# Gated convolution and GELU MLP, forward and backward: the MLP bias by full-row products or by ScalarE, smaller PSUM groups, and buffers laid out anew

## The chip, the cores and the metric

The kernel runs on one core of one Trainium2 chip. The metric is device time in microseconds for one execution, forward and backward together. TensorE is called PE below (PEld is its weight load), VectorE DVE, ScalarE ACT, GpSimd POOL, and SP is the engine whose queue issues most DMAs.

## What is computed

Four layers in a row on x of 2048 tokens by 512 channels, in bf16, and then all gradients of the chain. Layers 0 and 2 are a gated long convolution, layers 1 and 3 a GELU MLP; each acts on the layer norm of x and is added to x:

```
k_shift = 4-tap causal convolution of k;   kv = k_shift * v
A(n) = n * (causal convolution of kv with ssm_k, by FFT, + kv * ssm_D)
B(n) = gelu(n @ w1 + b1) @ w2 + b2          # w1 512x1376, w2 1376x512
x = x + A(ln(x)); x = x + B(ln(x)); x = x + A(ln(x)); x = x + B(ln(x))
out, grads = vjp of that chain for q, k, v, shift_k, ssm_k, ssm_D, w1, b1, w2, b2
```

A has the same k, v and filter in both layers, so its convolution is computed once.

## The kernel before, in words

The program has three stages. **The forward convolution** (`phase_conv_forward`) makes cosine and sine tables, turns k, v and the filter into spectra by products with the tables, multiplies them on DVE and transforms back; its result y stays in SBUF as `y_res`. At its end DVE adds y into x and sums the statistics of the first layer norm; POOL makes their reciprocal root (`rstd`, `nmr`).

**The MLP stage** (`phase_mlp`, L1605 on) takes x through all four layers and back. The tokens are cut into 8 blocks of 256 (`block_steps`); in each block there are two MLP layers forward (numbers 1 and 3) and two backward, so 16 block-layers each way. The hidden 1376 is padded to 11 chunks of 128. Forward (`mlp_layer`, L1213): ACT applies the norm (`l_n`), SP turns it by DMA (`l_nT`), PE forms each chunk in PSUM (`mm_ps`) with four products over 512 channels and a fifth that adds the bias, ACT copies the chunks to `l_g`, ACT and DVE compute gelu and its derivative in pieces of 6 and 5 chunks, the derivative goes to DRAM (`gp_d`), the hidden layer `l_h` goes to DRAM (`h_d`), and PE forms the second product in `oo_ps`. Before the change the fifth product has a contraction of one row: the weights are the row `b1` (`b_row` in the trace) and the moving operand a row of ones (`b_ones`):

```
for dc in range(ND):
    b_.nc.tensor.matmul(v, lhsT=w.w1[:, dc, cs], rhs=nT[:, dc, :], start=(dc == 0), stop=False)
b_.nc.tensor.matmul(v, lhsT=w.b1[:, cs], rhs=w.ones, start=False, stop=True)
```

The chunks are grouped by `ZG` (L1101): 3, 3, 3 and 2 chunks share a PSUM tile of 1024 columns, of which there are two, and one ACT copy takes a group out. Backward (`backward_layer`, L1297) works likewise with `w2T` and `w1T`, turned copies of the weights that `turn_steps` (L1105) makes at the stage's start, and ends each block with corrections of the layer norm on DVE, POOL and ACT; the last gradients of a block leave by SP (`out_dram`, `o1B_d`).

The order of that stage is not that of the code. `Plan` collects all steps with an estimated duration, a latency, and what they read and write; `Plan.order` (L1025) then places them one by one, each time the step that can start first by these estimates (ties by a rank with the constant `LEAN`), and hands out buffers from `SLOTS` (L1601). The program is emitted in that order, and each engine keeps its own.

**The rest** is the backward convolution (`conv_backward`) with the weight gradients (`weight_grads`) as a filler between its steps: it reads h from DRAM turned by DMA (`dw_tm`, 16 pieces of 128x128 each, `fetch` at L1485; the first five stand alone at L1534) and forms 22 sums of 32 products (`dw_ps`). The convolution loads its table (`tabFb`) and spectra (`Hb`, `KVb`); PE runs 61 products of `dw_ps` and then the first of the convolution (`sp_ps`). Tiles wait for whatever last used their place in SBUF, so where a tile lies decides what it waits for.

Of the kernel before, what the change touches and what calls it, by code (L numbers as in the profile page):

```python
# [16 lines left out]
P = 128  # L17
# [119 lines left out]
def build_consts(nc, tc, const_pool):  # L137
    c = Consts()
    with tc.tile_pool(name="c_tmp", bufs=1) as tp:
# [28 lines left out]
        nc.vector.memset(c.onescol_f, 1.0)  # L168
        c.pibias = const_pool.tile([P, 1], F32, name="pibias")
# [547 lines left out]
def conv_backward(ctx, nc, tc, dims, consts, dram, res, aps):  # L717
# [18 lines left out]
    with tc.tile_pool(name="cb_tabF", bufs=1, side="right", reuse_waits="tile") as tp:  # L736
        tabF = []
        for x, w in ((0, 512), (512, 1536)):
            tabF.append(tp.tile([P, 2, 2, w], BF16, name=f"tabFb{x}"))
            nc.scalar.dma_start(out=tabF[-1], in_=dram.tabF[:, :, :, x:x + w])  # L740
# [245 lines left out]
class Plan:  # L986
# [38 lines left out]
    def order(self, prio, ready_at, free):  # L1025
# [9 lines left out]
        open_ = {k: [(0.0, i) for i in range(n)] for k, n in self.slots.items()}  # L1035
# [21 lines left out]
        while len(out) < len(self.steps):  # L1057
# [29 lines left out]
def act_t(n, psum=False, cols=0):  # L1087
    return 0.05 + 0.835e-3 * n + 0.05 * psum + 0.1 * cols
# [6 lines left out]
def ts_t(n):  # L1095
    return 0.01 + 0.295e-3 * n
# [4 lines left out]
ZG = ((0, 3), (3, 3), (6, 3), (9, 2))  # L1101
EG = ((0, 6), (6, 5))


def turn_steps(p, m, E, A, consts):  # L1105

    D, ND, NFC, w = m.D, m.ND, m.NFC, m.w
    for dc in range(ND):
# [14 lines left out]
    for c in range(NFC):  # L1123
# [12 lines left out]
        E(1.1, mm, -1, 0, writes=[ps])  # L1136
        A(act_t(512, True), ev, -1, 0, reads=[ps], part=[("w1T",)])


def block_steps(p, m, dram, b, E, A, V, G, S, go_ap, out0, out1, forward):  # L1140
# [20 lines left out]
    def stats(l):  # L1161
        for i, t in enumerate(tl):
# [3 lines left out]
            V(0.68, f, b, l, reads=[X], part=[("mv", b)])  # L1166
# [7 lines left out]
        G(2.3, g, b, l, reads=[("mv", b)], writes=[("rs", b, l)])  # L1174
# [12 lines left out]
    def turned(N, key, l, src, hold, after=()):  # L1187
        for i in range(T):
# [3 lines left out]
            S(1.28, f, b, l, lat=1.7, reads=[N] if N else [], part=[key], hold=hold, after=after)  # L1192
# [20 lines left out]
    def mlp_layer(l):  # L1213
# [3 lines left out]
        hold = ("GE", b, l)  # L1217
# [4 lines left out]

        for c0, k in ZG:
            ps, gi = ("mm", b, l, c0), int(c0 >= EG[1][0])
            for c in range(c0, c0 + k):
                def f(b_, c=c, c0=c0, ps=ps):
# [51 lines left out]
        for i in range(T):  # L1278
# [18 lines left out]
    def backward_layer(l, first):  # L1297
# [16 lines left out]
        for gi, (g0, k) in enumerate(EG):  # L1314
            S(0.5, lambda b_, gi=gi, g0=g0, k=k, l=l, Q=Q: b_.nc.sync.dma_start(
                out=b_(Q[gi])[:, 0:k * HB], in_=m.gp_d[l][:, b, g0 * HB:(g0 + k) * HB]), b, st, lat=3.0,
              reads=[("gpd", b, l)], writes=[Q[gi]], after=[fed], hold=hold)
        for c0, k in ZG:
            ps = ("mm", b, l, c0, "B")
            for c in range(c0, c0 + k):  # L1320
# [6 lines left out]
                E(0.432, f, b, st, reads=[NT_, ("w2T",)], part=[ps], hold=hold)  # L1327
# [3 lines left out]
            A(act_t(k * HB, True), f, b, st, reads=[ps], part=[H + (int(c0 >= EG[1][0]),)], hold=hold)  # L1331
        H2 = [H + (0,), H + (1,)]
# [402 lines left out]
```

## Time and profile before

| | before |
|---|---|
| median of 3 runs (lowest to highest) | 950.11 us (945.30 to 954.85) |
| profiled execution, its own time | 939.36 us |
| its span in the trace | 937.6 us |
| busy: PE, DVE, ACT, POOL | 819.6, 744.1, 572.6, 185.8 us |
| granted TensorE clock, mean | 0.952 of full speed |

The span is the time from the first to the last instruction in the trace. A busy share is an average over stages with different limits. In rows of the timeline, the first number is the start and the second the duration; x4 means four instructions in one row, whose duration is from the start of the first to the end of the last. A row's bracket says how long the engine had been idle before it, and what ended that.

### The profile page before, as it was taken

The page shows a single profiled execution, that of the slowest core. Times are in us where ns is not written, and L with a number is a line of the kernel's source. Part 1 is how long each engine was busy: PE and PEld are TensorE (multiplying, and loading weights), DVE is VectorE, ACT ScalarE, POOL GpSimd, SP SyncE. Part 2 cuts the span into 40 slices and gives each one's busy share as a digit, 9 for nine tenths or more (in the row PEclk, how much of TensorE's full clock was granted, in tenths as well). Part 3 has the DMA queues.
Part 4 walks back from the last instruction along what each step waited for, and adds up shares of the span by engine and source line. Part 5 has one row for each costly group of instructions (what it writes and reads, how often), then busy time and mean ns, then how long its engine had stood idle before and what let it go on. Part 6 is the DMA issues. An engine that isn't in the chain of part 4 may idle for free. (4 is left out here: it accounts for less than half of the span.)

```text
span 937.6 us, 14102 instructions
## 1 busy us (share of the span) xinstructions
PE 819.6 (87%) x5282; PEld 452.2 (48%) x5282; DVE 744.1 (79%) x1289; ACT 572.6 (61%) x718; POOL 185.8 (20%) x329
## 2 busy tenths in 40 slices
PE   4778789348799999999999999786899998898997
PEld 4453334124343445555556566552344445765664
DVE  9865798962997877978997887787359999899774
ACT  7776645246778889788786765442433326754664
POOL 5401110110431210313231312222000122310000
PEclk9999989758896999999999999999999999999999
DMA  6788766031543455748576779959959999884321
GB/s 220 263 283 321 251 247 225 0 79 34 148 150 105 130 191 138 225 147 247 150 214 207 229 204 271 276 165 227 291 143 279 216 330 327 262 287 112 97 78 39
DMA packets 210030, 183.04 MB, mean 195 GB/s; under 512 B 94950, under 2 KB 184233, under 8 KB 209578
## 3 DMA queue, kind: packets, MB, share of 16 engines
q1 hardware_dynamic: 194762, 135.70, 50.8%
q0 software_dynamic: 11968, 40.15, 11.9%
q10 hardware_dynamic: 3232, 6.29, 1.8%
q8 instruction: 41, 0.67, 0.3%
q14 instruction: 27, 0.22, 0.1%
HBM read 86.32 MB, written 82.13 MB: 180 GB/s over the span
## 5 line engine op out<-in xcount | busy, mean ns | idle before, releaser
L55 ACT ACTIVATE l_g<-l_g 128x1536 bf16<-128x1536 bf16 (+1 forms) x96 | 128.7, 1370 | 5.2 <-DVE l_g L55 4.6
L55 PE MATMUL mm_ps<-l_nT,w_sb 128*128 128x256 bf16 x704 | 116.4, 292 | 3.4 <-ACT l_g L55 1.9
L55 PEld LDWEIGHTS <-l_h 128*128 128x128 bf16 x704 | 67.5, 99 | 99.5 <-DVE l_h L55 12.9
L55 PEld LDWEIGHTS <-dw_tm 128*128 128x128 bf16 x704 | 66.9, 99 | 83.5 <-DMA dw_tm<-h_d 8.0
L55 PEld LDWEIGHTS <-w_sb 128*128 128x128 bf16 x836 | 70.0, 102 | 70.0 <-issue 38.9
L55 PE MATMUL oo_ps<-w_sb,l_h 128*128 128x512 bf16 x352 | 85.3, 392 | 12.0 <-ACT w1T_sb L55 9.2
L55 PE MATMUL dw_ps<-G,dw_tm 128*128 128x512 bf16 x352 | 86.2, 384 | 7.3 <-DMA dw_tm<-h_d 3.7
L55 PE MATMUL dw_ps<-x_sl,dw_tm 128*128 128x512 bf16 x352 | 86.0, 385 | 3.5 <-DMA dw_tm<-h_d 3.5
L55 PE MATMUL mm_ps<-l_nT,w2T_sb 128*128 128x256 bf16 x704 | 82.2, 273 | 7.4 <-DMA l_nT<-goB_d 3.7
L55 DVE TENSOR_TENSOR l_g<-l_g,l_g 128x1536 bf16<-128x1536 bf16 (+1 forms) x96 | 83.5, 887 | 0.9
L55 PE MATMUL oo_ps<-w1T_sb,l_h 128*128 128x512 bf16 x352 | 80.0, 379 | 4.3 <-DVE l_h L55 4.2
L55 PEld LDWEIGHTS <-w2T_sb 128*128 128x128 bf16 x704 | 68.3, 98 | 21.9 <-issue 4.3
L55 ACT ACTIVATE l_g<-mm_ps 128x768 bf16<-128x768 f32 x64 | 48.3, 754 | 49.4 <-PE mm_ps L55 49.1
L55 ACT ACTIVATE l_h<-mm_ps 128x768 bf16<-128x768 f32 x64 | 47.6, 753 | 31.8 <-PE mm_ps L55 22.5
L55 DVE TENSOR_SCALAR l_g<-l_g 128x1536 bf16<-128x1536 bf16 (+1 forms) x64 | 33.3, 520 | 37.7 <-ACT l_g L55 37.7
L1506 ACT ACTIVATE dw_tm<-dw_tp 128x1024 bf16<-128x1024 bf16 x44 | 44.6, 1024 | 27.2 <-PE dw_tp L55 24.4
L55 PE MATMUL mm_ps<-b_ones,b_row 1*128 1x256 bf16 x176 | 51.3, 291 | 8.5 <-POOL b_ones L1628 8.5
L55 DVE TENSOR_REDUCE b1a<-dw_fm 128x1 f32<-128x2048 bf16 x22 | 49.6, 2277 | 0.0
L55 ACT ACTIVATE l_n<-x_sl,nmr,rstd 128x512 bf16<-128x512 bf16 x48 | 37.1, 806 | 18.4 <-POOL nmr L978 16.0
L55 POOL TENSOR_SCALAR l_dg<-ident,b_cols 128x128 bf16<-128x128 bf16 x32 | 25.5, 796 | 106.7 <-DVE b_junk L55 106.7
L1565 ACT ACTIVATE dw_o<-dw_ps 128x512 bf16<-128x512 f32 x22 | 13.1, 597 | 54.4 <-PE dw_ps L55 34.5
L55 ACT ACTIVATE l_n<-l_n,b_cols 128x512 bf16<-128x512 bf16 x32 | 24.8, 806 | 26.6 <-POOL b_cols L55 26.6
(296 smaller groups left out, 1559.6 us busy)
## 6 DMA issues: line engine op xcount, KB each, us to landing
h_d<-l_h SPq DMA_DIRECT2D x16, 704.0 KB, 4.8
gz_d<-l_h SPq DMA_DIRECT2D x16, 704.0 KB, 5.4
dw_fm<-gz_d SPq DMA_DIRECT2D x22, 512.0 KB, 9.0
l_n<-n_d SPq DMA_DIRECT2D x36, 256.0 KB, 5.0
n_d<-l_n SPq DMA_DIRECT2D x24, 256.0 KB, 3.3
gp_d<-l_g SPq DMA_DIRECT2D x16, 384.0 KB, 3.3
l_g<-gp_d SPq DMA_DIRECT2D x16, 384.0 KB, 3.8
gp_d<-l_g SPq DMA_DIRECT2D x16, 320.0 KB, 3.2
```

Of the source, the lines that this page charges most:

```text
L55: return self.tc.keep_in_program_order(f(*args, **kwargs))
L1506: nc.scalar.activation(out=dst, in_=ps, func=ACT.Identity)
L1565: nc.scalar.activation(out=o, in_=ps, func=ACT.Identity)
```

## The change

1. **Bias.** `BIAS_ROWS` names 9 of the 16 forward block-layers (layer 1 of blocks 0 to 4, layer 3 of blocks 0 to 3). There the fifth product stays, now with a full contraction: its weights are 128 rows of which the first is b1 and the rest zero, its moving operand a 128x256 tile of ones. In the other 7 it is gone, and ACT adds the bias while it copies, chunk by chunk, from a column `b1col`. The rows are cleared by ACT, and the column is made by 11 products of one column each; both are steps of the plan.
2. **PSUM groups.** `ZG` has groups of 2, 2, 2, 2, 2 and 1; `mm_ps` is four tiles of 512 columns. This holds for backward layers too.
3. **The plan.** Estimated durations are replaced; rank gets a number for each stage (`DELAY`); slots can be held back at the start (`LATE`) and are chosen by their number; `SLOTS` changes; some dependencies are narrowed.
4. **Places in SBUF.** The tiles of the MLP stage are laid out one by one in an order of their own. `tabFb` moves to the left side of SBUF, and `dw_t3`, `dw_t6` are taken last.

The diff, cut to what is spoken of:

```diff
+        c.ones = const_pool.tile([P, HB], BF16, name="ones")
+        nc.vector.memset(c.ones, 1.0)
...
-    with tc.tile_pool(name="cb_tabF", bufs=1, side="right", reuse_waits="tile") as tp:
+    with tc.tile_pool(name="cb_fold", bufs=1, side="right", reuse_waits="tile") as tp, \
+            tc.tile_pool(name="cb_tabF", bufs=1, reuse_waits="tile") as tabp:
...
-        open_ = {k: [(0.0, i) for i in range(n)] for k, n in self.slots.items()}
+        open_ = {k: [(LATE.get((k, i), -100.0), i) for i in range(n)] for k, n in self.slots.items()}
...
-ZG = ((0, 3), (3, 3), (6, 3), (9, 2))
+ZG = ((0, 2), (2, 2), (4, 2), (6, 2), (8, 2), (10, 1))
 EG = ((0, 6), (6, 5))
+BIAS_ROWS = {(b, 1) for b in range(5)} | {(b, 3) for b in range(4)}
...
+    def clear(b):
+        for f in range(0, FP, 256):
+            k = min(256, FP - f)
+            b.nc.scalar.activation(out=w.b1[:, f:f + k], in_=consts.nyq[:, 0:k], func=ACT.Copy, scale=0.0)
+        b.nc.scalar.activation(out=w.b1[0:1, F:F + 1], in_=consts.nyq[0:1, 0:1], func=ACT.Copy, scale=PAD_H)
...
+            b.nc.tensor.matmul(ps[:, c:c + 1], lhsT=w.b1[:, c * P:(c + 1) * P], rhs=consts.ones[:, 0:1], start=True, stop=True)
...
-                        b_.nc.tensor.matmul(v, lhsT=w.w1[:, dc, cs], rhs=nT[:, dc, :], start=(dc == 0), stop=False)
-                    b_.nc.tensor.matmul(v, lhsT=w.b1[:, cs], rhs=w.ones, start=False, stop=True)
-                forward.append(E(0.54, f, b, l, reads=[NT_], part=[ps], hold=hold))
+                        b_.nc.tensor.matmul(v, lhsT=w.w1[:, dc, cs], rhs=nT[:, dc, :], start=(dc == 0),
+                                            stop=(dc == ND - 1 and not by_row))
+                    if by_row:
+                        b_.nc.tensor.matmul(v, lhsT=w.b1[:, cs], rhs=consts.ones, start=False, stop=True)
+                forward.append(E(0.57 if by_row else 0.455, f, b, l, reads=[NT_, ("b1",)], part=[ps], hold=hold))
...
+                if by_row:
+                    b_.nc.scalar.activation(out=z, in_=v[:, 0:k * HB], func=ACT.Identity)
+                    return
+                for c in range(k):
+                    cs = slice(c * HB, (c + 1) * HB)
+                    b_.nc.scalar.activation(out=z[:, cs], in_=v[:, cs], func=ACT.Identity, bias=w.b1col[:, c0 + c:c0 + c + 1])
...
-    spare, held = [f"dw_t{x}" for x in range(7)], {}
+    spare, held = [f"dw_t{x}" for x in (0, 1, 2, 4, 5, 3, 6)], {}
...
-SLOTS = {"n": 5, "nT": 4, "h": 5, "g": 16, "u": 2, "gx": 5, "g1": 3, "dg": 4, "mm": 2, "oo": 4}
+SLOTS = {"n": 5, "nT": 4, "h": 5, "g": 17, "u": 2, "gx": 4, "g1": 1, "dg": 4, "mm": 4, "oo": 4}
-LEAN = 8.0
+LEAN = 10.7
+DELAY = (-0.2, 5.5, -10.9, 0.5, -1.8, -6.8, -0.8, 2.3, 6.2, 12.6)
...
-        nc.gpsimd.memset(m.w.ones, 1.0)
-        nc.gpsimd.memset(m.w.b1[:, F:NFC * P], 0.0)
-        nc.gpsimd.memset(m.w.b1[:, F:F + 1], PAD_H)
...
-        tiles["mm"] = [psum.tile([P, 1024], F32, name=f"mm_ps{i}") for i in range(SLOTS["mm"])]
+        tiles["mm"] = [psum.tile([P, 512], F32, name=f"mm_ps{i}") for i in range(SLOTS["mm"])]
```

What this does to the engines' orders shows at two places. The first is ACT at the start of the MLP stage, from the last copy of the forward convolution (`W`) on; `w2T_sb` are the copies of turned weights, `l_n` the first two norms. Before:

```order
L371 ACTIVATE W_1389<-iv_ps 128x512
L55 ACTIVATE l_n_1933<-x_sl,nmr_101,rstd_98 128x512 x2
L55 ACTIVATE l_n_1934<-x_sl,nmr_101,rstd_98 128x512 x2
L55 ACTIVATE w2T_sb<-oo_ps_1979 128x1024
L55 ACTIVATE w2T_sb<-oo_ps_1980 128x1024
L55 ACTIVATE w2T_sb<-oo_ps_1981 128x1024
L55 ACTIVATE w2T_sb<-oo_ps_1982 128x1024
L55 ACTIVATE w2T_sb<-oo_ps_1979 128x384
```

The same place on ACT in the changed kernel, where `b_rows` is the clearing of the bias rows:

```order
L373 ACTIVATE W_1391<-iv_ps 128x512
L55 ACTIVATE b_rows<-nyq 128x256 x5
L55 ACTIVATE b_rows<-nyq 128x128
L55 ACTIVATE b_rows<-nyq 1x1
L55 ACTIVATE w2T_sb<-oo_ps_1971 128x1024
L55 ACTIVATE w2T_sb<-oo_ps_1972 128x1024
L55 ACTIVATE w2T_sb<-oo_ps_1973 128x1024
L55 ACTIVATE w2T_sb<-oo_ps_1974 128x1024
L55 ACTIVATE w2T_sb<-oo_ps_1971 128x384
```

The clearing and the copies of turned weights, seven of which stood behind the first norms, now all stand ahead of them. The second place is SP's queue at the end of the MLP stage, before:

```order
L55 DMA gz_d<-l_h_1945 1408x1x256
L55 DMA l_n_1937<-n_d 128x2x512
L55 DMA out_dram<-l_n_1935 128x2x512
L1491 DMA_TRANSPOSE dw_tm<-h_d 128x16x128 x5
L55 DMA o1B_d<-l_n_1937 128x2x512
L55 DMA_TRANSPOSE dw_tm<-h_d 128x16x128 x3
```

And the same end of SP's queue in the changed kernel:

```order
L55 DMA gz_d<-l_h_1962 1408x1x256
L55 DMA l_n_1958<-n_d 128x2x512
L55 DMA out_dram<-l_n_1956 128x2x512
L55 DMA o1B_d<-l_n_1958 128x2x512
L1525 DMA_TRANSPOSE dw_tm<-h_d 128x16x128 x5
L55 DMA_TRANSPOSE dw_tm<-h_d 128x16x128 x3
```

The store of the last block's gradient (`o1B_d`) moved ahead of the first five turned loads of h.

## Rows read from the trace of the kernel before

**Rows 1.** Busy time by stretch: span; PE, PEld, DVE, ACT, POOL busy (count); clock; DMA.

```profile
186.00:205.00 19.00, 5.21 (x25) 2.55 (x25) 15.68 (x31) 7.71 (x11) 3.03 (x8) 0.50 0.39 97
205.00:240.00 35.00, 26.21 (x139) 12.67 (x139) 12.36 (x18) 24.22 (x26) 0.00 (x0) 0.74 0.12 32
240.00:545.00 305.00, 294.83 (x1761) 159.45 (x1760) 253.45 (x456) 242.87 (x284) 76.78 (x124) 0.97 0.60 178
545.00:641.00 96.00, 83.38 (x530) 50.70 (x529) 77.78 (x182) 48.88 (x66) 22.70 (x48) 1.00 0.81 228
641.00:664.00 23.00, 17.34 (x66) 7.13 (x67) 11.96 (x15) 2.12 (x3) 4.17 (x7) 0.85 1.06 279
664.00:938.00 274.00, 257.93 (x1841) 148.74 (x1839) 223.18 (x322) 136.92 (x199) 36.67 (x49) 1.00 0.70 201
```

**Rows 2.** Waits of DVE and ACT from 240 to 641 us: total, times, longest.

```profile
DVE l_g L55 <- ACT l_g L55: 20.4, 18, 2.6
...
ACT l_g L55 <- PE mm_ps L55: 28.1, 28, 3.8
```

**Rows 3.** Timeline of PE: two forward chunks, and a backward layer's 44 products.

```profile
219.91 0.61 PE L55 MATMUL mm_ps<-l_nT,w_sb 128*128 128x256 bf16 x4
...
220.66 0.61 PE L55 MATMUL mm_ps<-l_nT,w_sb 128*128 128x256 bf16 x4
...
575.73 4.97 PE L55 MATMUL mm_ps<-l_nT,w2T_sb 128*128 128x256 bf16 x44
580.53 0.59 PE L55 MATMUL oo_ps<-l_n,l_dg 128*128 128x512 bf16 x2
```

**Rows 4.** Timeline and groups of ACT by shape: count | busy us, mean ns | idle.

```profile
239.80 2.02 ACT L55 ACTIVATE w1T_sb<-oo_ps 128x512 bf16<-128x512 f32 x4
...
L55 ACT ACTIVATE l_g<-mm_ps 128x768 bf16<-128x768 f32 x48 | 38.7, 807 | 38.8 <-PE mm_ps L55 38.5
L55 ACT ACTIVATE l_n<-x_sl,nmr,rstd 128x512 bf16<-128x512 bf16 x48 | 37.1, 806 | 18.4 <-POOL nmr L978 16.0 <-POOL nmr L55 2.3
L55 ACT ACTIVATE l_g<-mm_ps 128x512 bf16<-128x512 f32 x16 | 9.6, 597 | 10.6 <-PE mm_ps L55 10.6
...
L893 ACT ACTIVATE Wh<-gh_ps 128x257 bf16<-128x257 f32 x24 | 8.0, 386 | 3.6 <-PE gh_ps L55 3.6
```

**Rows 5.** Timeline of the MLP stage's start, several engines.

```profile
186.59 2.93 ACT L55 ACTIVATE l_n<-x_sl,nmr,rstd 128x512 bf16<-128x512 bf16 x4 [16.01 <-POOL nmr L978]
...
192.56 1.06 PE L55 MATMUL mm_ps<-l_nT,w_sb 128*128 128x256 bf16 x4
...
199.28 2.74 DVE L55 TENSOR_TENSOR y_res<-W 128x512 bf16<-128x512 bf16 x8
...
202.08 0.37 PE L55 MATMUL mm_ps<-b_ones,b_row 1*128 1x256 bf16 x1 [8.46 <-POOL b_ones L1628]
...
211.27 0.56 DVE L55 TENSOR_SCALAR l_g<-l_g 128x1536 bf16<-128x1536 bf16 x1 [9.25 <-ACT l_g L55]
...
240.42 3.92 PE L55 MATMUL oo_ps<-w_sb,l_h 128*128 128x512 bf16 x11 [9.21 <-ACT w1T_sb L55]
```

**Rows 6.** Timeline of the MLP stage's end: SP's queue, PE, DVE.

```profile
637.63 16.24 SPq L1491 DMA_TRANSPOSE dw_tm<-h_d  x5
...
643.20 5.01 PE L55 MATMUL dw_ps<-G,dw_tm 128*128 128x512 bf16 x16 [3.73 <-DMA dw_tm<-h_d]
...
646.70 0.69 DVE L55 TENSOR_TENSOR l_n<-l_u,l_n 128x1024 bf16<-128x1024 bf16 x1 [1.06 <-ACT l_n L55]
...
658.58 4.67 PE L55 MATMUL dw_ps<-x_sl,dw_tm 128*128 128x512 bf16 x13 [3.46 <-DMA dw_tm<-h_d]
663.05 1.92 PE L55 MATMUL sp_ps<-fold_t,tabFb 128*128 128x512 bf16 x8
```

**Rows 7.** Busy time in two stretches of 5 us, columns as in rows 1.

```profile
285.00:290.00 5.00, 5.00 (x21) 2.11 (x20) 3.51 (x5) 4.68 (x6) 0.63 (x3) 0.50 0.43 110
...
585.00:590.00 5.00, 1.29 (x8) 0.44 (x6) 4.93 (x13) 0.00 (x0) 2.52 (x3) 1.00 1.23 299
```

More of the change, by code (lines that the diff above doesn't have):

```diff
@@ L1068, in order @@
                 if n not in held:
-                    open_[n[0]].sort()
-                    held[n] = open_[n[0]].pop(0)[1]
+                    got = [x for x in open_[n[0]] if x[0] <= t + 1e-6]
+                    got = max(got, key=lambda x: x[1]) if o.stage > 4 else min(got, key=lambda x: x[1])
+                    open_[n[0]].remove(got)
+                    held[n] = got[1]
             free[o.eng] = t + o.dur
@@ L1191, in f @@
                 b_.nc.sync.dma_start_transpose(out=v[:, :, i * P:(i + 1) * P], in_=src(b_, i))
-            S(1.28, f, b, l, lat=1.7, reads=[N] if N else [], part=[key], hold=hold, after=after)
+            S(1.28, f, b, l, lat=2.0, reads=[N] if N else [], part=[key], hold=hold, after=after)
     def forward_layer(l):
@@ L1216, in mlp_layer @@
         turned(N, NT_, l, lambda b_, i, N=N: half(b_(N))[:, i, :], ("LN", b, l))
-        hold = ("GE", b, l)
+        holds = [("GE", b, l, 0), ("GE", b, l, 1)]
         def part(a, gi, c0, c1):
@@ L1300, in backward_layer @@
         Q = [("g", b, l, "B", gi) for gi in range(2)]
-        hold = ("GZ", b, l)
+        H2 = [("half", b, l, gi) for gi in range(2)]
+        hold, came = ("GZ", b, l), []
         if first:
-            S(0.5, lambda b_: b_.nc.sync.dma_start(out=half(b_(GX)), in_=io_ap(go_ap, dram.goB)), b, st, lat=3.0,
-              writes=[GX], after=[last], hold=hold)
+            came.append(S(0.5, lambda b_: b_.nc.sync.dma_start(out=half(b_(GX)), in_=io_ap(go_ap, dram.goB)), b, st,
+                          lat=3.0, writes=[GX], after=[last], hold=hold))
             def src(b_, i):
@@ L1380, in backward_layer @@
             if first:
-                V(0.67, f, b, st, reads=[ps], writes=[] if i else [GX], part=[GX] if i else [])
+                V(0.67, f, b, st, reads=[ps], part=[GX], after=came)
             else:
@@ L1396, in f @@
                                                   op1=ALU.mult, accum_out=cols[:, 2, i:i + 1])
-            V(STT_T, f, b, st + 1, reads=[GO], writes=[] if i else [U], part=[U] if i else [], hold=ab)
+            V(STT_T, f, b, st + 1, reads=[GO], part=[U], writes=[("ut", b, la, i)], hold=ab)
         def f(b_, N=N, GO=GO):
@@ L1422, in backward_layer @@
                 bias=cols[:, 2, i:i + 1]),
-              b, st + 1, reads=[("ab", b, la)], writes=[] if i else [N], part=[N] if i else [], hold=ab)
+              b, st + 1, reads=[("ab", b, la)], part=[N], hold=ab)
         if first:
```

101 lines of the change are left out of this document (62 added, 39 removed).

## Prediction

> **What bounds the kernel now.** I read the busy time by stretch first, since each stage has its own limit. From 240 to 545 us, the middle of the MLP stage, PE is busy 294.8 of 305 us (96.7%), DVE 253.5 (83%), ACT 242.9 (80%) [rows 1]. The list of waits says who follows whom: DVE waits for ACT's copies to `l_g`, 20.4 us in 18 waits, and ACT for PE's chunks in `mm_ps`, 28.1 us in 28 [rows 2]. So PE sets the pace there, and the other two have 52 and 62 us to spare. From 545 to 641 nobody is full (PE 83.4 of 96, DVE 77.8): the last blocks wait for one another. At the start, 186 to 240, PE works 31.4 of 54 us at clocks of 0.50 and 0.74. From 641 to 664 DMA is full (1.06) and PE has 17.3 of 23; from 664 to 938 PE has 257.9 of 274 (94%) [rows 1], so what is late at 664 makes the end late.
>
> **Part one, the bias on PE.** Two forward chunks follow each other at 219.91 and 220.66: 0.75 us for four products and one bias product [rows 3]. Elsewhere 44 products take 580.53 − 575.73 = 4.80 us, 0.109 each, so four take 0.437 [rows 3], and the product with one row takes 0.75 − 0.44 = 0.316, three times a full one. There are 16 × 11 = 176 chunks. After the change 99 have a full-row bias product, which the trace doesn't show for this use; its bounds are 0.109 (any full product here) and 0.316 (no gain from more rows). I take 0.109, since weights and moving operand have the shape of the 44. A chunk is then 0.546, and the 77 without bias 0.437: Two block-layers, 22 chunks of the first kind, stand before 240; of the 154 after it 77 are of each kind: 154 × 0.753 = 116.0 us become 77 × 0.546 + 77 × 0.437 = 75.7, and PE's 294.8 become 254.5. With the product at 0.316 only the other 77 gain, 24.3, and they become 270.5.
>
> The Trainium skill, page "TensorE: Matmul & The Clock Gate", section "Why this matters for your kernels", says that a single product with a short contraction takes the time of a full one. By that only the 77 dropped products save anything, 77 × 0.109 = 8.4 us, which in the stretch at 96.7% would be worth 9 and leave about 938 for the median, all else as below. By the row it isn't so here: 0.75 a chunk isn't 5 × 0.109 = 0.546; I give that case no chance.
>
> **Part two, the copies on ACT.** Groups of two chunks in place of three mean more copies. A copy of 768 columns takes 807 ns, one of 512 columns 597 [rows 4]: 0.82 ns a column and about 0.18 fixed. Four copies of 512 in a row take 2.02 us, so they follow each other every (2.02 − 0.59)/3 = 0.477 [rows 4], 0.12 less than their durations. With that overlap a block-layer whose bias comes by rows goes from 3 × 0.69 + 0.48 = 2.55 to 5 × 0.477 + 0.27 = 2.65 (the same holds for 16 backward ones): 25 × 0.1 = 2.5 us. For the 7 with a bias column it is 11 copies of 256 columns. 257 columns take 386 ns alone [rows 4], 0.27 in a row; a pointer operand costs (0.806 − 0.597)/2 = 0.105 by the norm that has two [rows 4]; 11 × 0.375 = 4.1, 1.6 more than now: 11 us. Sum +14 us on ACT (by the durations without overlap 0.35 × 25 + 2.4 × 7 ≈ 25), 242.9 becomes about 257. Clearing the rows and making the column cost nothing: ACT idles 16.01 us before its first norm at 186.59, for POOL's `nmr` [rows 5], and the clearing stands there; if that cover went, it is seven ACT instructions, under 3 us.
>
> **The middle.** PE 254.5, ACT 257 and DVE 253.5 (its work is unchanged but for one memset) are now alike, and none has the room that lets it run at 96.7%. The bounds: at 96.7% the stretch is 266 (−39); if it can't beat DVE's present 83% it is about 305 (0, or +4 with ACT's additions). Three equal engines that feed one another by four small PSUM tiles come out between; PE's own density in the last part, 94%, is nearest [rows 1], less a little for the coupling: 92%, so 257/0.92 = 279, **−26 us**. With the full-row product at 0.316, PE at 270.5/0.967 = 280 gives the same, so that term hardly matters. Not counted: DVE's 20.4 us of waits for ACT may grow, as ACT now does 11 small copies where it did four; that is inside the 92%. From 545 to 641 I take nothing (−6 to +3): latencies hold there, and `l_g1` with one buffer is taken and freed once a block.
>
> **The start.** PE has its first four products at 192.56, then waits 8.46 us until 202.08 for `b_ones`, a POOL memset queued behind POOL's part of the norm [rows 5]. That operand goes: the ones are made in the constants. At 0.50 clock a product costs 2 × 0.109, five 1.09, the six chunks of the first piece 6.5: from 192 or a little before they end at 198.6, copy and square at 200.3. DVE is in its adds into `y_res` until 202.02 [rows 5], and is what is late next: first gelu at 202.1 rather than 211.27 [rows 5], **−9 us**. Bounds: −11 if DVE's adds stand behind; 0 if PE's next wait, 9.21 us at 240.42 for ACT's copies of `w1T` [rows 5], swallows it. The `w2T` copies that now stand ahead of the norms on ACT are covered by the same 16 us.
>
> **The end.** SP issues the five turned loads of h from 637.63, in 16.24 us, 3.25 each [rows 6]. Now the store of `o1B_d` stands ahead of them. It waits for DVE's last add to `l_n`, 646.70 + 0.69 = 647.4 [rows 6], and behind it on SP wait all `dw_tm` loads, for which PE waits: 3.73 us at 643.20 and 3.46 at 658.58 [rows 6]. So the first load starts some 10 us later. PE's products on the first two go from before 643 to after 655; the fourth load is issued at 648 + 4 × 3.25 = 661 and lands by about 664 to 666, if its flight is as at 658.58; its 13 products take 4.7, and `sp_ps` starts at 667 to 671 rather than 663.05: **+6 us**, bounds +3 (part of it hidden by DMAs that no longer crowd: the share is 1.06 today) and +10 (the whole shift). What follows is PE's 94% stretch, and shifts whole. `tabFb`'s new place matters little: its load can be issued sooner, but it isn't what comes last.
>
> **Sum.** −9 − 26 + 6 = −29 us on the profiled execution's 939.4 (span 937.6 and 1.8 around it), so 910. That execution lies 10.7 below the median of the three runs, which spread over 9.5 us themselves; I put the difference on the median: 950.1 − 29 = **921**.
>
> **Rivals.** A measurement of this kernel can tell about 1% (9.5 us) from no change.
>
> *All engines keep 96.7%.* PE alone had that, because the others had room; for it speaks that the plan places every step anew. −39 in the middle, −9, +6, and a little of the last blocks (−4): 904.
>
> *DVE's waits are latencies.* In it PE isn't what holds DVE at 83%; the chain copy, square, gelu, product does, whose steps don't shrink. For it: from 545 to 641 PE has room (87%) and DVE still has only 81% [rows 1]. Against: of ACT's waits 28.1 us are for PE's chunks [rows 2]. Middle 0, so −9 + 0 + 6 = −3: 947.
>
> *PE's clock falls between its bursts.* PE's clock isn't always full in the middle: from 285 to 290 PE is busy 5.00 of 5 us at a granted clock of 0.50, which is the level of 1.2 GHz, while from 585 to 590 it does 1.29 us at 1.00, 2.4 GHz [rows 7]. The mean of 0.97 over 305 us [rows 1] makes some 18 us at the lower level (305 × 0.03/0.5), which cost 9. With PE idle for short times between groups of two chunks there may be more such patches. At 279 us PE has 279 − 254 = 25 to spare, which pays for three; from there each costs 9 in full. The time of before is reached at (29 + 25)/9 = 6 patches, from where it decides; at eight it is slower, 921 + 72 − 25 = 968. Against: the last blocks run at 87% with a clock of 1.00 [rows 1], so idle times alone don't lower it.
>
> The Trainium skill, same page, section "A second HAM failure mode: psum-queue depth-cycling", describes this: PE's short idles between groups through cycling PSUM banks make the clock swing between its two levels. By that rule the changed kernel is the slow case, 968; by the rows at 585 to 590 it is not.
>
> **How the numbers follow.** The forecast, 921, has 0.68; all at 96.7%, 904, has 0.10; latencies, 947, 0.15; the clock, 968, 0.07. The range leaves out the clock case and the ends of the others: 899 (middle −39 with the start's −11) to 942 (middle −13, start and end at their bad bounds, or a milder form of the latency case). Faster by over 1% (under 940.6): 0.68 and 0.10 and a little of the latency case, 0.80; within 1%: most of the latency case, 0.11; slower by over 1%: the clock case and a bad tail, 0.09.
>
> **What would show it.** Right: PE's forward chunks start 0.546 apart where the bias product stands and 0.437 where it doesn't; no wait for `b_ones`, and DVE's first gelu 9 us sooner against its last `y_res` add; PE, DVE and ACT all near 90% in the middle, PE's busy time down by about 40; and from PE's last product of the MLP stage to the first `sp_ps` some 6 us more than now, with PE waiting for `dw_tm`. Wrong: chunks at 0.75 with the full-row product (then the rows cost what they did); DVE still at 83% with ACT's waits for `mm_ps` gone (latencies); a clock row with several fives between 240 and 640; or PE at 97% with DVE and ACT idle, if a plan that had room for all three left PE bound still.

## The result: 6.6% faster, and where it came from

The changed kernel took 885.8 us (median of 4) against 947.7 for the kernel before: a ratio of 0.934, with an interval of 0.925 to 0.942. One of its executions took 909.2 us, the other three 883.9 to 885.8. The forecast was 921 with a range of 899 to 942, so the gain, 62 us, was about twice the 29 that were forecast. The two profiled executions have spans of 937.6 and 883.9 us, 53.7 apart; that difference is accounted for here (the one of before lies some 8 us below its median).

The stages are now cut at events instead of at round times: PE's first product of the MLP stage, its first second product, its last product of the stage, the first `sp_ps`, the end. Columns as in rows 1. The kernel before:

```profile
192.56:240.42 47.86, 30.19 (x155) 14.32 (x154) 21.97 (x40) 26.37 (x31) 2.48 (x7) 0.68 0.20 56
240.42:639.47 399.05, 378.21 (x2290) 210.15 (x2289) 329.36 (x631) 291.33 (x349) 99.48 (x172) 0.98 0.65 190
639.47:663.05 23.58, 16.39 (x62) 6.65 (x63) 13.45 (x19) 2.12 (x3) 4.17 (x7) 0.86 1.05 278
663.05:937.60 274.55, 258.88 (x1845) 149.22 (x1843) 223.18 (x322) 136.92 (x199) 36.67 (x49) 1.00 0.70 201
```

The changed kernel, the same four cuts:

```profile
191.46:217.25 25.79, 20.86 (x169) 16.07 (x170) 22.04 (x43) 21.15 (x27) 2.56 (x5) 0.90 0.42 118
217.25:573.20 355.95, 333.86 (x2206) 214.42 (x2205) 326.83 (x631) 300.39 (x448) 107.98 (x172) 0.99 0.73 212
573.20:609.14 35.94, 16.02 (x61) 6.71 (x62) 13.54 (x19) 2.11 (x3) 3.60 (x6) 0.67 0.82 212
609.14:883.90 274.76, 258.85 (x1845) 149.19 (x1843) 223.24 (x322) 136.82 (x199) 37.10 (x50) 1.00 0.66 197
```

The start lost 22.1 us, the long stretch 43.1, the end gained 12.4, and what follows is the same. The first product also came 1.1 us sooner. In the long stretch PE's busy time fell by 44.3 and its idle time hardly moved: 399.05 − 378.21 = 20.8 before, 355.95 − 333.86 = 22.1 after. DVE is now busy 92% of it and ACT 84%. Of the waits of that stretch, those between ACT and DVE and of ACT for PE became shorter. PE's wait for ACT's copies of chunks became longer, the first line before, the others after the change:

```profile
PE mm_ps L55 <- ACT l_g L55: 1.9, 2, 1.1
```

```profile
DVE l_g L55 <- ACT l_g L55: 9.0, 9, 2.3
...
PE mm_ps L55 <- ACT l_g L55: 6.0, 7, 2.6
...
PE oo_ps L55 <- ACT w1T_sb L55: 3.3, 1, 3.3
...
ACT l_g L55 <- PE mm_ps L55: 2.8, 4, 1.4
```

[rows 2], from 240 to 641 us, had 20.4 us for the first and 28.1 for the last of these four. The timeline of the changed kernel, rows that answer to [rows 3, 5, 6]:

```profile
199.73 0.60 PE L55 MATMUL mm_ps<-l_nT,w_sb 128*128 128x256 bf16 x4
200.17 0.27 PE L55 MATMUL mm_ps<-ones,b_rows 128*128 128x256 bf16 x1
200.28 0.60 PE L55 MATMUL mm_ps<-l_nT,w_sb 128*128 128x256 bf16 x4
...
202.01 0.95 DVE L55 TENSOR_SCALAR l_g<-l_g 128x1536 bf16<-128x1536 bf16 x2
...
217.25 3.90 PE L55 MATMUL oo_ps<-w_sb,l_h 128*128 128x512 bf16 x11 [3.29 <-ACT w1T_sb L55]
...
359.12 2.78 PE L55 MATMUL mm_ps<-l_nT,w_sb 128*128 128x256 bf16 x24
361.74 2.54 PE L55 MATMUL oo_ps<-w_sb,l_h 128*128 128x512 bf16 x11
...
581.14 0.36 SPq L55 DMA_DIRECT2D o1B_d<-l_n  x1
581.56 18.52 SPq L1525 DMA_TRANSPOSE dw_tm<-h_d  x5
...
593.12 6.47 PE L55 MATMUL dw_ps<-G,dw_tm 128*128 128x512 bf16 x16 [19.93 <-DMA dw_tm<-h_d]
...
609.14 1.89 PE L55 MATMUL sp_ps<-fold_t,tabFb 128*128 128x512 bf16 x8
```

A chunk with a full-row bias product takes 200.28 − 199.73 = 0.55 us from start to start, one without about 0.44 (24 products of six chunks from 359.12 to the next product at 361.74). The first gelu stands at 202.01. At the end the store waits until 581.14, the turned loads of h behind it, and PE 19.93 us for them.

### The profile page after: what moved, and what is told of

Its sections match the earlier page's. It is cut to its first block, busy times and chain, and to the rows that moved or that the text cites. A ratio compares the mean times of both kernels' runs of the same rounds, so it can differ in the third digit from the quotient of the medians.

```text
span 883.9 us, 14073 instructions
## 1 busy us (share of the span) xinstructions
PE 766.2 (87%) x5216; PEld 458.4 (52%) x5216; DVE 740.9 (84%) x1290; ACT 580.4 (66%) x825; POOL 194.0 (22%) x326
## 5 line engine op out<-in xcount | busy, mean ns | idle before, releaser
L55 ACT ACTIVATE l_g<-l_g 128x1536 bf16<-128x1536 bf16 (+1 forms) x96 | 131.6, 1396 | 3.0 <-DVE l_g L55 2.5
L55 PE MATMUL mm_ps<-l_nT,w_sb 128*128 128x256 bf16 x704 | 94.6, 279 | 21.8 <-DMA l_nT<-l_n 14.6
L55 PEld LDWEIGHTS <-w_sb 128*128 128x128 bf16 x836 | 79.6, 99 | 49.0 <-issue 30.2
L55 PE MATMUL oo_ps<-w_sb,l_h 128*128 128x512 bf16 x352 | 82.7, 384 | 6.5 <-ACT w1T_sb L55 3.3
L55 ACT ACTIVATE l_h<-mm_ps 128x512 bf16<-128x512 f32 x96 | 49.8, 584 | 12.3 <-PE mm_ps L55 12.2
L55 ACT ACTIVATE l_n<-x_sl,nmr,rstd 128x512 bf16<-128x512 bf16 x48 | 37.1, 827 | 13.2 <-POOL nmr L981 8.8
L55 ACT ACTIVATE l_n<-l_n,b_cols 128x512 bf16<-128x512 bf16 x32 | 25.6, 835 | 20.5 <-POOL b_cols L55 20.5
L55 DVE TENSOR_SCALAR l_g<-l_g 128x1280 bf16<-128x1280 bf16 (+1 forms) x64 | 32.6, 522 | 7.2 <-ACT l_g L55 5.6
L55 POOL TENSOR_SCALAR rstd<-ln_mvs 128x2 f32<-128x2 f32 x20 | 13.9, 696 | 100.6 <-DVE ln_mvs L55 100.4
L55 DVE TENSOR_TENSOR l_h<-l_g,l_g 128x1536 bf16<-128x1536 bf16 (+1 forms) x32 | 28.4, 889 | 8.0 <-ACT l_g L55 7.9
```

The costliest lines, as they stand in the source:

```text
L55: return self.tc.keep_in_program_order(f(*args, **kwargs))
```

## The experiments

Eighteen runs, each one edit away from the kernel before, the changed kernel or another experiment. The table has each ratio to the kernel before (of the runs made beside it) and, from each profile, the three parts of the MLP stage at the same events: the start, the stretch (first second product to last product) with PE's idle time in it, and the end.

| kernel | ratio (interval) | start | stretch | PE idle in it | end |
|---|---|---|---|---|---|
| before | 1 | 47.9 | 399.1 | 20.8 | 23.6 |
| e1_early | 0.992 (0.988 to 0.996) | 41.4 | 398.0 | 22.9 | 24.6 |
| e2_early_rows | 0.974 (0.965 to 0.983) | 36.6 | 386.3 | 36.6 | 36.1 |
| e3_again | 0.963 (0.957 to 0.969) | 33.4 | 381.9 | 36.6 | 21.3 |
| e4_ranks | 0.988 (0.982 to 0.993) | 33.7 | 400.2 | 45.7 | 26.7 |
| changed | 0.934 (0.925 to 0.942) | 25.8 | 356.0 | 22.1 | 35.9 |
| a1_onerow | 0.954 (0.947 to 0.961) | 37.9 | 361.2 | 15.1 | 35.6 |
| a3_allrows | 0.938 (0.935 to 0.942) | 25.5 | 354.6 | 13.2 | 34.8 |
| a4_act | 0.946 (0.942 to 0.950) | 25.6 | 361.8 | 31.7 | 34.4 |
| a5_groups | 0.967 (0.962 to 0.973) | 25.7 | 379.4 | 44.0 | 35.6 |
| a6_oldplan | 0.958 (0.952 to 0.963) | 31.8 | 368.0 | 32.9 | 34.5 |
| f1_dur | 0.961 (0.954 to 0.968) | 27.4 | 381.2 | 38.6 | 36.3 |
| f2_places | 0.948 (0.939 to 0.956) | 34.3 | 354.5 | 20.8 | 39.6 |
| f3_hold | 0.949 (0.942 to 0.956) | 25.9 | 367.5 | 29.2 | 35.1 |
| f4_slots | 0.969 (0.962 to 0.976) | 22.3 | 390.1 | 44.0 | 35.1 |
| g1_lean | 0.941 (0.938 to 0.945) | 25.5 | 360.4 | 23.4 | 35.2 |
| g2_round | 0.951 (0.946 to 0.955) | 25.4 | 371.5 | 30.9 | 34.6 |
| a2_tail | 0.923 (0.916 to 0.930) | 25.6 | 353.7 | 18.8 | 19.2 |
| a7_tail2 | 0.924 (0.919 to 0.929) | 25.7 | 355.7 | 24.1 | 19.3 |

In the traces of a5_groups, a6_oldplan and a7_tail2 some 30 products lack a record (2170, 2157 and 2178 stand beside 2200, 2190 and 2205 weight loads), which makes their idle times some 3 to 7 us too high, at 0.11 to 0.22 us each. The three parts of a row come from one execution. Executions of one kernel can lie several us apart (e2_early_rows took 913.9 to 926.8), so a difference of a few us between two rows shows nothing by itself. The kernel before had a median of 947.7 us beside the changed kernel and of 942 to 946 beside the others; where a run is close to the changed kernel, the medians are compared as well.

### The bias, from the kernel before

```diff
-        nc.gpsimd.memset(m.w.ones, 1.0)
-        nc.gpsimd.memset(m.w.b1[:, F:NFC * P], 0.0)
-        nc.gpsimd.memset(m.w.b1[:, F:F + 1], PAD_H)
+        nc.scalar.activation(out=m.w.ones, in_=consts.nyq[0:1, 0:HB], func=ACT.Square)
+        for f in range(0, NFC * P, HB):
+            k = min(HB, NFC * P - f)
+            nc.scalar.activation(out=m.w.b1[:, f:f + k], in_=consts.nyq[0:1, 0:k], func=ACT.Copy, scale=0.0)
+        nc.scalar.activation(out=m.w.b1[0:1, F:F + 1], in_=consts.nyq[0:1, 0:1], func=ACT.Copy, scale=PAD_H)
...
```

> The kernel before, with one edit: the ones and the rest of the bias row are made by ACT in its idle time ahead of the first norms instead of by POOL behind them; order of the plan, groups and the one-row bias product stay. Theory start (the wait for b_ones held everything behind it): first gelu on DVE at about 202 instead of 211.3, first second product 9 to 17 us sooner, the kernel 9 to 12 us faster, 936 to 939 against 948. Rival (PE's later wait for the w1T copies swallows it): 0 to 3 us faster.

`e2_early_rows` has the same lines with 128 rows in place of one.

> As e1_early, and the bias product with a full contraction (128 rows, all but the first zero) in all 16 forward block-layers; the order of the plan, the groups of three and two PSUM tiles stay as before the change. Theory work (PE sets the pace all through the MLP stage and the others have room): 176 x (0.316 - 0.109) = 36 us less PE work, time falls by all of it, 34 to 38 us below e1_early. Rival room (without the new order and four PSUM tiles DVE and ACT, at 83 and 80 per cent, take over): 10 to 20 us below e1_early.

The two cuts of e1_early, then of e2_early_rows:

```profile
193.76:235.16 41.40, 29.59 (x155) 14.27 (x154) 21.96 (x40) 26.25 (x31) 2.08 (x4) 0.71 0.24 64
235.16:633.17 398.01, 375.13 (x2290) 209.99 (x2289) 329.28 (x631) 291.00 (x349) 99.98 (x172) 0.98 0.65 190
```

```profile
192.05:228.69 36.64, 21.41 (x156) 15.82 (x155) 21.97 (x40) 26.04 (x31) 2.08 (x4) 0.83 0.27 73
228.69:615.02 386.33, 349.71 (x2290) 225.31 (x2289) 328.55 (x631) 288.30 (x349) 102.41 (x172) 0.97 0.67 196
```

The wait for `b_ones` was worth 0.8%, 7.5 us, a little under its theory's 9 to 12, and nearly all of it in the start. The first gelu came at 206.37 us, not at the 202 expected: ACT's first copy of chunks waited for DVE's last adds into `y_res`, as the trace of e1_early has it:

```profile
203.31 1.51 ACT L55 ACTIVATE l_g<-mm_ps 128x768 bf16<-128x768 f32 x2 [7.83 <-DVE y_res L55]
```

The full rows took 375.13 − 349.71 = 25.4 us of PE's work out of the stretch, of which only 11.7 became time: PE's idle time rose from 22.9 to 36.6. The medians are 17.5 us apart (934.4 and 916.9). So in the order of before the theory of room holds and that of work falls. (The end of e2_early_rows has 36.1 us because PE waited 15.5 for the fourth turned load in the profiled execution, which took 926.8 against a median of 916.9.)

### The bias, from the changed kernel

```diff
-                        b_.nc.tensor.matmul(v, lhsT=w.b1[:, cs], rhs=consts.ones, start=False, stop=True)
+                        b_.nc.tensor.matmul(v, lhsT=w.b1[0:1, cs], rhs=consts.ones[0:1, :], start=False, stop=True)
```

> The changed kernel, with the contraction of its 99 bias products cut back to one row; order and everything else stay. Theory work: 99 x 0.207 = 20.5 us more PE work, 18 to 21 us slower than the changed kernel, about 905. Rival room (DVE, busy 91 per cent in the stage, is the bound of the changed kernel): PE has 25 us to spare, 3 to 10 us slower.

The cuts of a1_onerow, two pieces of its start, and two chunks of its stretch:

```profile
190.78:228.66 37.88, 36.90 (x169) 16.18 (x169) 22.13 (x43) 21.93 (x27) 2.56 (x5) 0.58 0.29 80
228.66:589.89 361.23, 346.14 (x2206) 207.59 (x2205) 327.62 (x631) 301.39 (x448) 107.28 (x172) 1.00 0.73 209
...
200.00:205.00 5.00, 5.00 (x21) 2.03 (x20) 1.87 (x6) 1.89 (x3) 0.99 (x3) 0.50 0.01 3
...
215.00:220.00 5.00, 5.00 (x29) 2.16 (x29) 1.90 (x3) 2.99 (x5) 0.00 (x0) 0.50 0.75 192
...
250.97 0.61 PE L55 MATMUL mm_ps<-l_nT,w_sb 128*128 128x256 bf16 x4
...
251.72 0.61 PE L55 MATMUL mm_ps<-l_nT,w_sb 128*128 128x256 bf16 x4
```

And one piece of the changed kernel's:

```profile
200.00:205.00 5.00, 5.00 (x49) 4.49 (x47) 4.56 (x11) 4.97 (x9) 1.68 (x3) 1.00 0.05 9
```

The MLP stage grew by 17.4 us, near what the theory of work wanted, but not where it wanted it; the medians, 900.0 and 885.8, are 14 apart, between the two theories. 77 of the 99 products lie in the stretch, 77 × 0.207 = 15.9 us. PE's busy time grew by 12.3 there (the mean clock was 1.00 instead of 0.99), and the stretch by only 5.3, idle falling from 22.1 to 15.1: there the theory of room fits, with DVE at 92% in the changed kernel. The other 12.1 us are in the start, for 22 products of 4.6 us: with one-row products PE stayed at a granted clock of 0.50, its level of 1.2 GHz, to beyond 220 us, busy 36.9 of 37.9 us all the while; with full rows it was at 1.00 from 200 on. No run tells whether a one-row product is slow by itself or because it stands between products with a full contraction.

Next, who adds the bias, with the order unchanged: a3_allrows puts a full-row product in all 16 block-layers (`if by_row` becomes `if True` at the product and at the copy), a4_act leaves it in two (`rows_ = l == 1 and b < 2` in its place).

> The changed kernel with the full-row bias product in all 16 forward block-layers and plain copies on ACT in all; the order stays. PE has 77 x 0.109 = 8.4 us more work, ACT about 11 us less. Theory work (PE alone sets the time): 8 us slower than the changed kernel. Rival room (PE has some 10 us to spare behind DVE once the start is over, as a1_onerow's later stretch grew by 5 us for 16 us of work): within 3 us of it.

> The changed kernel with the bias added by ACT in all block-layers but the first two (14 instead of 7); the order stays. PE has 77 x 0.109 = 8.4 us less work, ACT some 11 us more, in blocks where it is busy 93 to 97 per cent (240 to 440 us). Theory work: 8 us faster than the changed kernel. Rival room: ACT's copies come later there, 3 to 10 us slower.

a3_allrows can't be told from the changed kernel (medians 884.8 and 885.8 us; stretch 354.6 and 356.0): its 7.5 us more of PE work came out of PE's idle time, 22.1 to 13.2. With a4_act PE's wait for ACT's copies more than doubled, the stretch grew by 5.9, and the median is 6.2 above that of the changed kernel:

```profile
PE mm_ps L55 <- ACT l_g L55: 13.7, 13, 2.8
```

So the theory of room again, both times; that ACT adds the bias in 7 block-layers is worth nothing that can be measured here.

### The order: groups, ranks, durations, buffers

The idle time of 36.6 us in e2_early_rows against 22.1 in the changed kernel, for less PE work, was what the bias didn't explain. a5_groups and e3_rows_groups move the groups alone (with the number and size of the `mm_ps` tiles), a6_oldplan and e4_ranks the ranks alone. The diff is that of a5_groups and a6_oldplan, from the changed kernel; e3_rows_groups (from e2_early_rows) and e4_ranks (from e3_rows_groups) go the other way:

```diff
-ZG = ((0, 2), (2, 2), (4, 2), (6, 2), (8, 2), (10, 1))
+ZG = ((0, 3), (3, 3), (6, 3), (9, 2))
...
-LEAN = 10.7
-DELAY = (-0.2, 5.5, -10.9, 0.5, -1.8, -6.8, -0.8, 2.3, 6.2, 12.6)
+LEAN = 8.0
+DELAY = (0.0,) * 10
```

> The changed kernel with the groups of before: 3, 3, 3 and 2 chunks, two PSUM tiles of 1024 columns; the plan is worked out again with its new numbers, biases as changed. PE's work is the same. Asked: what keeps PE fed once the bias is cheap (idle in the MLP stage 52 us in e2_early_rows, 27 in the changed kernel). Theory tiles (four small tiles): 15 to 25 us slower than the changed kernel, 897 to 907. Rival plan (the new order): 0 to 5 us slower.

> The changed kernel with the ranks of before in the plan (LEAN 8, no DELAY), everything else as changed; PE's work is the same. Theory plan (the stages' delays give the order that keeps PE fed): 15 to 25 us slower than the changed kernel, idle of PE in the MLP stage near 50 us. Rival tiles: 0 to 5 us slower.

> e2_early_rows (before, full-row bias, start freed) with the groups of two chunks and four PSUM tiles of 512 columns; the plan is worked out again with the numbers of before. Theory tiles: 15 to 25 us below e2_early_rows, 892 to 902. Rival plan (the tiles alone are worth little): 3 us below to 5 above, 914 to 922.

> e3_rows_groups once more, word for word the same kernel, since its profile and two of its times were disturbed. Theory tiles alone are worth nothing in the old plan: median 912 to 920 and an MLP stage of 415 to 425 us. Rival (they are worth some 10 us): 902 to 910 and 408 to 414.

> e3_rows_groups with the ranks of the changed kernel in the plan (LEAN 10.7 and DELAY); buffers, durations and places as before the change. Theory ranks (the order by DELAY with four tiles is what feeds PE): MLP stage 15 to 20 us shorter than in e3_rows_groups. Rival (the ranks fit only the new durations and buffers): within 5 us of it, or longer.

The four times of e3_rows_groups lay far apart (904, 912, 920 and 2046 us; ratio 0.964), so it was run again as e3_again (0.963). The long stretch of e3_again and of a5_groups:

```profile
225.87:607.81 381.94, 345.30 (x2306) 224.24 (x2305) 329.75 (x634) 292.84 (x411) 102.13 (x172) 0.98 0.69 199
```

```profile
218.79:598.16 379.37, 335.41 (x2170) 214.73 (x2200) 327.38 (x630) 298.79 (x402) 102.32 (x171) 0.98 0.69 199
```

In the old order four small tiles shorten the stretch by 4.4 us and the start by 3.2, in one execution each; the medians are 916.9 and 910.6. This lies between the two expectations. In the new one the old groups cost 23.4 in the stretch and the old ranks 12.1: both theories were right there, and the two sums do not add up to anything, for the new ranks in the old arrangement (e4_ranks) made the stretch 18.2 us longer. So four more parts were taken back one at a time. f1_dur has the durations and latencies of before in the plan, f2_places the tiles in their old sequence in SBUF (the plan unchanged), f3_hold one hold for both pieces of a forward layer, and f4_slots the old numbers of buffers:

```diff
-        holds = [("GE", b, l, 0), ("GE", b, l, 1)]
+        holds = [("GE", b, l)] * 2
...
-SLOTS = {"n": 5, "nT": 4, "h": 5, "g": 17, "u": 2, "gx": 4, "g1": 1, "dg": 4, "mm": 4, "oo": 4}
+SLOTS = {"n": 5, "nT": 4, "h": 5, "g": 16, "u": 2, "gx": 5, "g1": 3, "dg": 4, "mm": 4, "oo": 4}
```

> The changed kernel with the plan's durations and latencies of before (all numbers in the steps and in the two formulas), ranks, groups, buffers and places as changed. Theory durations (the ranks are fitted to them): 15 to 25 us slower than the changed kernel, like old ranks. Rival (the order is robust against a few hundredths of a us): within 5 us.

> The changed kernel with the MLP stage's tiles laid in SBUF in the sequence of before (turned weights first, then the buffers by kind); the plan is the same. Theory places (tiles that lie over the convolution's wait for it at the stage's start): the first gelu or the first second product 5 to 10 us later, 5 to 10 us slower. Rival: within 3 us, the convolution's last tiles are free by then.

> The changed kernel with one hold for both pieces of a forward layer (its buffers of l_g are taken together, as before the change). Theory holds: the plan finds less room for forward layers, 5 to 15 us slower. Rival: within 3 us.

> The changed kernel with the numbers of buffers of before (l_g 16, l_gx 5, l_g1 3); the plan is worked out again. Theory buffers (the seventeenth l_g gives the gelu room): 5 to 15 us slower. Rival: within 3 us, or faster, since l_g1 has three again.

f2_places is the one with a clean mechanism, since its order is that of the changed kernel. Its cuts, and ACT's first copy of chunks in it and then in the changed kernel:

```profile
191.80:226.07 34.27, 22.52 (x168) 16.81 (x169) 22.21 (x43) 21.31 (x27) 2.56 (x5) 0.83 0.32 88
226.07:580.60 354.53, 333.73 (x2206) 214.36 (x2205) 326.73 (x631) 300.21 (x448) 110.51 (x172) 0.99 0.75 213
...
202.52 1.08 ACT L55 ACTIVATE l_g<-mm_ps 128x512 bf16<-128x512 f32 x2 [12.61 <-DVE y_res L55]
```

```profile
193.79 0.60 ACT L55 ACTIVATE l_g<-mm_ps 128x512 bf16<-128x512 f32 x1 [4.21 <-PE mm_ps L55]
```

The stretch is the same, the start 8.5 us longer: in the old places ACT's first copy waits for DVE's last adds into `y_res`, and the first gelu stands at 207.64 instead of 202.01. The other three made the stretch 25, 12 and 34 us longer; the buffers (f4_slots) cost twice the most that was expected. By then the parts taken back came to more than the whole gain, which suggested that each edit just threw away one good order. Two last kernels test that with edits that mean nothing: LEAN 10.5 (g1_lean), and DELAY rounded to whole us (g2_round).

> The changed kernel with LEAN 10.5 instead of 10.7, nothing else: another order of the same instructions, with no mechanism of its own. Theory fit (the numbers pick one good order, and a neighbour is an ordinary one): stretch from the first second product to the last product of the MLP stage 365 to 385 instead of 356 us, 10 to 28 us slower than the changed kernel. Rival (each part taken back has a cause of its own; a neighbouring number changes little): within 4 us.

> The changed kernel with the ten DELAY numbers rounded to whole us, nothing else. Theory fit: 10 to 28 us slower than the changed kernel, with PE's idle time in the MLP stage 35 to 50 us instead of 27. Rival: within 4 us.

The long stretch of g2_round:

```profile
218.61:590.09 371.48, 340.54 (x2206) 216.11 (x2205) 326.50 (x631) 300.28 (x448) 105.22 (x172) 0.98 0.70 203
```

g1_lean has a stretch 4.4 us longer, but its profiled execution is the slowest of its four, and its median, 885.7 us, is that of the changed kernel (885.8): no loss is shown, as the rival had it. g2_round lost 15.5 in the stretch, with PE's wait for ACT's copies at 9.3 us; three of its executions took 894.1 to 900.3. Of two neighbouring orders one thus costs nothing and one as much as old ranks (12.1) or one hold (11.5): of these two no more can be said than that the order may be fitted to them. Old groups, durations and buffers (23 to 34) lie above both neighbours, though two are few to know the spread by; why each costs so much was not settled. Not taken back alone were the slots held back at the start (`LATE`), the narrowed dependencies, and the new places of `tabFb` and the `dw_t` tiles.

### The end

```diff
-        S(0.5, lambda b_, N=N: b_.nc.sync.dma_start(out=io_ap(out1, dram.o1B), in_=half(b_(N))), b, st + 1, lat=3.0,
-          reads=[N], hold=ab)
+        S(0.5, lambda b_, N=N: (b_.nc.scalar if b == 7 else b_.nc.sync).dma_start(
+            out=io_ap(out1, dram.o1B), in_=half(b_(N))), b, st + 1, lat=3.0, reads=[N], hold=ab)
```

> The changed kernel, with the last block's o1B store issued by ACT instead of SP, so that the first five turned loads of h don't stand behind it. Theory queue (the wait of PE of 19.9 us at the end is the store's wait for the last corrections): the loads start at about 572 instead of 581.6, first sp_ps 9 to 10 us sooner, 876 to 877 against 886. Rival (the loads are held by DMA bandwidth or by their places in SBUF): 0 to 3 us faster.

a7_tail2 has `b >= 6` in that place.

> a2_tail with the store of the last but one block issued by ACT too, so that the turned loads of h stand behind no store. Theory queue: they start at about 565.6 instead of 569.1, PE's first wait for them (4.2 us) goes, 3 to 4 us below a2_tail, 867 to 868 against 871. Rival (the fourth load and the DMA share of 1.11 set the end of that wait, whenever they start): 0 to 1 us.

The end of a2_tail:

```profile
569.13 19.70 SPq L1525 DMA_TRANSPOSE dw_tm<-h_d  x5
...
574.48 5.15 PE L55 MATMUL dw_ps<-G,dw_tm 128*128 128x512 bf16 x16 [4.19 <-DMA dw_tm<-h_d]
...
578.68 1.55 ACTq L743 DMA_DIRECT2D tabFb<-tabF_d  x2
...
589.46 1.89 PE L55 MATMUL sp_ps<-fold_t,tabFb 128*128 128x512 bf16 x8
```

The end shrank from 35.9 to 19.2 us, more than the 9 to 10 expected, and is now shorter than the 23.6 of before: the loads begin 1.2 us ahead of the end of PE's last product (570.29) instead of 8.4 behind it, and PE waits for them once, 4.19 us. The first product on a turned load also comes 5.4 us after the loads' issue, and not 11.6 as in the changed kernel. The median was 871.2 us, 0.923 of the kernel before. The intervals of the two ratios meet, but the slowest execution of a2_tail, 873.2, lies 10.7 us below the fastest of the changed kernel. The second store brought nothing (19.3 us, 0.924), as the rival had it. These two are the fastest versions that were run (871.2 and 869.8 us).

## Why the prediction was wrong

The direction held, and two steps of the sum fell short: the middle by 17 us and the start by 13. The end took 6 more than forecast: −29 − 17 − 13 + 6 = −53. That is 24 of the 35 us between 921 and 885.8. The other 11 are the base: the forecast put the 10.7 us between the profiled execution of before and the median of its three runs on the median, but the changed kernel's profiled execution, 885.75, lies at its median, and in later runs the kernel before had medians of 942 to 946.

**The bias on PE: right.** Chunks of 0.55 and 0.44 us, as worked out. PE's busy time in the stretch fell by 44.3, near the forecast of 40.3; its mean clock there rose from 0.98 to 0.99, which works the same way.

**The middle: the density of 92% failed.** The step read that three engines near 255 us would "come out between", 92%, and so gave back 14 of the 40 us as new idle time of PE, while the last blocks got nothing. In the stretch as a whole, PE's density was 94.8% before and 93.8% after, and the time fell by 43.1 instead of 26. The last 530 products of the stretch begin at 545 us before and near 485 after; cut there, the changed kernel has

```profile
217.25:485.00 267.75, 253.12 (x1673) 163.03 (x1673) 251.52 (x465) 244.95 (x357) 90.20 (x129) 0.99 0.70 202
485.00:573.20 88.20, 80.74 (x536) 51.39 (x533) 75.30 (x167) 55.44 (x92) 17.78 (x44) 1.00 0.82 242
```

PE, DVE and ACT are alike, as forecast, but busy 95, 94 and 91% of the middle, all at once: it took 268 us, not 279. The last blocks, for which the sum had nothing, gave the other 6. The step describes what the old order does: e2_early_rows has 90.5%, and 25.4 us of work became 11.7 of time. The planned order with its four tiles was taken for a detail of the same density; what came with it is worth the larger part. From e3_again, which has the full rows and four tiles, to the changed kernel (ranks, durations, buffers, holds, places, and 7 block-layers' bias on ACT) the stretch fell by 26.0, of which PE's smaller work was 11.4 and idle time 14.5. Which of these makes the order good, and how, stays open. That the plan places every step anew was named for the first rival, 904, which had 0.10; its terms for this stretch, −39 and −4, add up to the −43 that was measured.

**The start: right in its number, partly by luck, and stopped too early.** The first gelu was forecast at 202.1 and stood at 202.01, 9.3 us sooner and right behind DVE's adds, as described. But the step gave all of it to the wait for `b_ones`. With nothing but that wait taken away it came at 206.37 (e1_early), and with the tiles in their old places at 207.64 (f2_places): in both, ACT's first copy waits for DVE's adds, and the new places, which the step counted for nothing, let it go ahead. And the stage goes on to its first second product, which came 23.2 us sooner. From the first gelu it took 29.2 us before and 15.2 after, of which the sum counted nothing; the bad bound, 0, was for a wait there, and the good one, −11, stops at the gelu. From the kernel before, taking the wait for `b_ones` away shortens the start by 6.5 us (e1_early) and the full rows with the clock by 4.8 more (e2_early_rows). From the changed kernel, one-row products lengthen it by 12.1 (a1_onerow), the old places by 8.5 (f2_places) and the old ranks by 6.0 (a6_oldplan). The two sets don't add up to the 22.1; what a part is worth hangs on the others.

**The end: right in kind, twice the size.** Forecast +6, bounds +3 to +10, measured +12.4. The store held the loads as described (a2_tail shows it by taking it away): against the end of PE's last product of the stage they were issued 10.2 us later. What failed is that the step let the loads flow as before once issued, and `tabFb`'s new place matter little. The first product on a turned load came 11.6 us after their issue, 5.6 before the change. The 2 MB of `tabFb` were issued 14.2 us behind the turned loads, and now 2.6 us ahead of them, and the DMA share is 1.01 right behind that. First the kernel before, then the changed kernel:

```profile
651.86 1.27 ACTq L740 DMA_DIRECT2D tabFb<-tabF_d  x2
```

```profile
578.97 1.26 ACTq L743 DMA_DIRECT2D tabFb<-tabF_d  x2
...
581.50:584.50 3.00, 0.00 (x0) 0.00 (x0) 2.90 (x2) 0.00 (x0) 0.00 (x0) 0.50 1.01 328
```

That this traffic made the loads slow is read from the order: in a2_tail the loads are ahead of `tabFb` again and the 11.6 us are 5.4, but no run moves `tabFb` alone. PE's clock isn't the reason. It was lower in the mean over the end (0.67, 0.86 before), but PE's products took no longer, 16.0 us against 16.4.

**ACT's term was too large.** +14 was worked out for the middle, to 257; it has 245 there by the cut above, and in the whole stretch ACT's busy time went from 291.3 to 300.4 us. The term raised the base of the density from 254.5 to 257, which is worth under 3 us.

**The rivals.** Latencies that hold DVE at 83%: wrong, DVE is at 92%. PE's clock falling between its bursts: wrong, the mean over the stretch is 0.99. So the rule of the Trainium skill, "TensorE: Matmul & The Clock Gate", section "A second HAM failure mode: psum-queue depth-cycling", isn't borne out here by four cycling tiles. The rule of the Trainium skill, same page, section "Why this matters for your kernels", that a single product with a short contraction takes the time of a full one (it names 32 rows), doesn't hold for one row behind four full products, by a1_onerow as by [rows 3]: in its stretch two chunks follow each other by 0.75 us where the changed kernel has 0.55.

## What to carry to other kernels

When an engine that sets the pace loses work, ask twice: how much of it the order at hand can turn into time (here less than half), and whether the change also brings another order; the price of an order can't be read from engine sums, and of two neighbours of one that was fitted by numbers one lost nothing and one 15 us, so that an ablation of it can measure the loss of the fit as much as that of the part. Follow a stall that goes to the end of its stage, not to the next instruction. And a store at the end of one stage belongs on a queue on which the next stage's loads don't stand: here moving it took 16.8 us out of the end, some of it perhaps because the loads then also stood ahead of the tables.

## What was not expected of the hardware

The one-row product can cost more than its own time. In the kernel before PE had been idle 1.15 us at 283, the clock fell, and then came eleven chunks with such a product, without a gap:

```profile
285.03 1.03 PE L55 MATMUL mm_ps<-l_nT,w_sb 128*128 128x256 bf16 x4
286.00 0.39 PE L55 MATMUL mm_ps<-b_ones,b_row 1*128 1x256 bf16 x1
286.32 1.03 PE L55 MATMUL mm_ps<-l_nT,w_sb 128*128 128x256 bf16 x4
...
296.61 4.84 PE L55 MATMUL oo_ps<-w_sb,l_h 128*128 128x512 bf16 x11
```

A chunk takes 1.29 us there, at a granted clock of 0.50 [rows 7], the level of 1.2 GHz; the clock came back, to 2.4 GHz, only during the second products at 296.61, which have none. In the changed kernel a fall after 2.56 us of idle time at 373 was over by 380 (0.86 and 0.80 over the two pieces of 5 us). With a1_onerow, where PE stayed at 0.50 for some 30 us of the start though it was always busy, beside the changed kernel, at 1.00 from 200 on, both late rises stand in stretches of one-row products. The start of a1_onerow is 12.1 us longer, for 4.6 us of added work at the full clock. In the long stretch it isn't shown: the patch of 17 us is gone from the changed kernel, but a1_onerow, with one-row products, has a mean clock of 1.00 there, and e2_early_rows, with full rows, 0.97, less than the 0.98 of before.
